# A new hand-set order of all engines, new PSUM banks and single-timed late weight loads in an attention and soft-MoE kernel

## Chip, cores and metric

The kernel runs on one core of one Trainium2 chip. The metric is device time in microseconds (us) of one execution; three executions of the kernel before gave a median of 356.9 us (354.47 to 360.94).

## What is computed

Eight batches with eight heads of 576 tokens and 64 channels go through block-causal attention (blocks of 64), and the result, as 4608 rows of 512, through a soft mixture of 8 experts with 4 slots each. All data are float32.

```python
scores = where(block_i >= block_j, q @ k.T / 8, -1e9)
x = softmax(scores) @ v                        # 4608 x 512
logits = x @ phi                               # 4608 x 32
slot_input = softmax(logits, axis=0).T @ x     # 32 x 512, over all rows
slot_out[e] = relu(slot_input[e] @ w1[e]) @ w2[e]
out = softmax(logits, axis=1) @ slot_out
```

The maximum over all rows makes a barrier: the experts start when the last batch has given its logits.

## The kernel before

**Two stages.** Stage one, up to about 299 us, is attention in 32 pairs of heads (4 pairs a batch, numbered 0 to 31) and, batch by batch, the logits and a running sum for the slots. Stage two, from `up` (L959) on, is the two expert layers and the output. The change touches stage one and the weight loads between the two.

**A pair.** The 576 rows of a pair's two heads are cut into tiles by how many key columns they may see: two tiles "7" of 512 columns (70 and 71, one for each head), two tiles "5" of 384 (50, 51), and the small ones "8" (576), "3" (256), "2" (192), "1" (128) and "0" (64). Its steps are:

- loads of k, q and v on SP (`load_k` L406, `load_q` L402, `load_v` L413 and L417), each into one of two areas that alternate by pair; k is scaled on POOL (L423)
- scores on PE: `qk` for the tiles 7 and 5 (L459), `qkb` for the others (L480)
- masked maximum on DVE (`rowmax`, L494 for tiles 7 and 5, L499 for the rest); exponential with its row sum on ACT (`expo`, L509)
- epsilon on POOL (`zeps`, L520) and reciprocal on DVE (`zinv`, L516), in three groups of tiles: 70 and 71, then 8 to 0, then 50 and 51; product with the reciprocal on POOL (`norm`, L527)
- 50 transposes on PE (`tr`, L547) in four groups g7 (16), g5 (12), gc (10, tile 8) and gd (12, tiles 3 to 0), each group into two PSUM banks, copied out by ACT (L389) or DVE (L391)
- product with v on PE (`pv` L579, `pv8` L589), copied out as x

**Once a batch.** PE makes the logits (L607, L614), 40 transposes of x (`xnat`, L716), 3 of the weights (`natural`, L666) and the slot sums (`slots` L736, `slots4` L745); POOL keeps the running maximum (L642, L645).

**What sets the order.** Every step is entered with a time, `at(t, fn, ...)`; the steps are sorted by time, and each engine gets its instructions in that order. The times are numbers in a table `TM` by step and place in the batch (`.0` to `.3`; letters for the first six and last three pairs). They only order; at run time an instruction goes when its semaphores allow, and an engine does not pass a waiting one. A table `EN` says which engine copies (v DVE, a ACT), a table `BK` which of the eight PSUM banks a step uses.

```python
  448          def scores(x, m):
...
  858          for t, _, fn, args in sorted(ops, key=lambda o: o[:2]):
  859              fn(*args)
```

**Weights.** 32 pieces of 1 MB. Pieces 0 to 16 go to places of their own during stage one, at times 1.6 pairs apart (L826). Pieces 17 to 23 (the late pieces) go over areas of attention that have ended (L846 to 854), the others over pieces that stage two has used.

Of the kernel before, what the change touches and what calls it, by code (L numbers as in the profile page):

```python
# [45 lines left out]
for name, n in (  # L46
# [58 lines left out]
    62.5406, "elg": 65.9472, "stats": 66.7664, "stats1": 67.0993, "stats2": 69.737, "enl": 82.2887, "ndt": 74.5616,  # L105
    "disp": 74.9226, "disp2": 135.6855, "xq0": 74.0947, "en0a": 75.0227, "en0b": 75.1964, "xq1": 62.9684, "en1a":
    65.1834, "en1b": 65.4166, "xn4": 65.4755, "en4a": 65.8907, "en4b": 65.8745, "sl": 90.1991, "sl4": 88.8341,
    "sacc": 91.9687, "sacc4": 90.0509, "lkA": -97.9102, "lqA": -56.266, "ksA": -73.6468, "lkB": -53.518, "lqB":
# [6 lines left out]
    -5.3661, "nm51A": -0.1355, "UBB": -7.3076, "gcA": 11.0108, "egcA": 13.7334, "ogcA": 13.9553, "rm8B": -6.9664,  # L115
# [6 lines left out]
    11.3725, "ex50B": 4.9925, "paA": 26.8907, "xbA": 26.6199, "ex51B": 4.1693, "xaA": 27.4575, "lqD": -20.3083,  # L122
# [128 lines left out]
def tile_attention_softmoe(  # L251
# [805 lines left out]
```

## Time and profile before

| what | value |
|---|---|
| median of three executions | 356.9 us (354.47 to 360.94) |
| profiled execution, its own time | 353.48 us |
| its span from first to last instruction | 351.4 us |
| PE busy | 333.5 us, 95% of the span |
| DVE, ACT, POOL busy | 269.8, 258.0, 205.9 us |
| mean granted TensorE clock | 0.992 |

Busy time is the union of an engine's instructions. A matmul's end is modelled, so the time from the start of one step to the start of the next says more than the length of a row. In the order lists below, one row is an instruction with its output, its input and the shape.

### The profile page before, as it was taken

How to read it: one execution, taken by the hardware profiler on the slowest of the kernel's cores; microseconds unless marked ns; L12 is line 12 of the kernel's file. 1: busy time of each engine (PE TensorE's matmuls, PEld its weight loads, DVE VectorE, ACT ScalarE, POOL GpSimd, SP SyncE). 2: the span in 40 equal slices, each digit the busy share in tenths (PEclk: the TensorE clock that was granted, in tenths of full speed). 3: DMA queues.
4: the chain of work that ended last, by engine and by line, in shares of the span. 5: the costliest groups of instructions: out<-in, count | busy, mean ns of one | idle time of the engine just before them, and what ended most of it. 6: DMA issues, size and time to landing. Idle time of an engine off the chain costs nothing.

```text
span 351.4 us, 14291 instructions
## 1 busy us (share of the span) xinstructions
PE 333.5 (95%) x5664; PEld 231.7 (66%) x5664; DVE 269.8 (77%) x816; ACT 258.0 (73%) x855; POOL 205.9 (59%) x475
## 2 busy tenths in 40 slices
PE   8899899999999999999999999799999999999990
PEld 4567577776767677768666777576767686347660
DVE  6899868989789869977898799678988856463352
ACT  4978968888988898878987898589878975032341
POOL 4887838867685768666866686567774862100000
PEclk9999999999999999999999999999999999999996
DMA  5766546385266453762565534823331139999988
GB/s 168 226 248 234 143 183 190 103 288 191 71 216 202 163 187 108 258 220 71 172 224 187 187 106 165 306 78 100 118 120 41 37 122 423 422 427 425 415 344 337
DMA packets 28930, 72.28 MB, mean 206 GB/s; under 512 B 6848, under 2 KB 15168, under 8 KB 23872
## 3 DMA queue, kind: packets, MB, share of 16 engines
q1 hardware_dynamic: 28864, 71.38, 57.1%
q8 instruction: 44, 0.72, 0.9%
q14 instruction: 22, 0.18, 0.1%
HBM read 61.93 MB, written 9.44 MB: 203 GB/s over the span
## 4 chain that ended last, share of the span: by engine, by line
PE 76%; DMA 7%; DVE 5%; POOL 5%; ACT 3%; issue 2%; SPq 1%; DVEq 0%; POOLq 0%
PE ps L579 16%; PE ps L547 14%; PE ps L459 12%; PE ps L480 8%; DMA arena<-in_v 6%; PE ps L589 5%; PE so L984 4%; PE hp L964 4%; POOL arena L527 4%; PE ps L716 3%; ACT arena L509 3%; PE o L935 3%; PE ps L607 2%; DVE ps L494 2%; PE ps L736 2%
## 5 line engine op out<-in xcount | busy, mean ns | idle before, releaser
L509 ACT ACTIVATE arena<-ps,stat 128x384 f32<-128x384 f32 (+6 forms) x288 | 152.7, 543 | 30.5 <-DVE stat L494 23.6
L527 POOL TENSOR_SCALAR arena<-arena,stat 128x384 f32<-128x384 f32 (+6 forms) x288 | 152.0, 544 | 31.4 <-DVE stat L516 19.6
L494 DVE CUSTOM_DVE_ANT_1 ps<-ps,mask 128x512 f32<-128x512 f32 (+1 forms) x128 | 76.5, 649 | 6.4 <-PE ps L459 5.1
L391 DVE COPY arena<-ps 128x384 f32<-128x384 f32 (+3 forms) x136 | 69.7, 548 | 15.1 <-PE ps L547 4.9
L579 PE MATMUL ps<-arena 128*64 128x256 f32 (+2 forms) x640 | 76.1, 384 | 2.7 <-DMA arena<-in_v 2.6
L389 ACT COPY arena<-ps 128x384 f32<-128x384 f32 (+3 forms) x140 | 62.7, 514 | 11.9 <-PE ps L547 7.6
L547 PE MATMUL ps<-ident,arena 64*128 64x64 f32 x1600 | 64.9, 227 | 1.7 <-POOL arena L527 0.9
L547 PEld LDWEIGHTS ps<-ident,arena 64*128 64x128 f32 x1600 | 57.0, 139 | 11.2 <-POOL arena L527 2.9
L579 PEld LDWEIGHTS ps<-arena 128*64 128x64 f32 x640 | 41.7, 137 | 32.9 <-issue 18.3
L509 ACT ACTIVATION_READ_ACCUMULATOR arena<-ps,stat 128x1 f32 x288 | 59.6, 207 | 0.0
L459 PE MATMUL ps<-arena 64*128 64x384 f32 (+1 forms) x256 | 58.7, 558 | 0.7 <-DMA arena<-in_q 0.4
L499 DVE TENSOR_REDUCE stat<-ps 128x1 f32<-128x128 f32 (+4 forms) x160 | 56.3, 401 | 3.4 <-PE ps L480 2.7
L480 PEld LDWEIGHTS ps<-arena 64*64 64x64 f32 x768 | 36.2, 132 | 21.1 <-ACT arena L389 8.6
L520 POOL TENSOR_SCALAR stat<-stat 128x2 f32<-128x2 f32 (+1 forms) x96 | 18.9, 197 | 48.5 <-ACT arena L509 44.5
L480 PE MATMUL ps<-arena 64*64 64x288 f32 (+4 forms) x768 | 42.9, 340 | 0.4 <-ACT arena L509 0.3
L459 PEld LDWEIGHTS ps<-arena 64*128 64x128 f32 x256 | 24.6, 187 | 15.2 <-issue 5.2
L589 PE MATMUL ps<-arena 128*64 128x64 f32 x640 | 24.9, 224 | 1.7 <-DMA arena<-in_v 1.7
L391 DVE COPY xn<-ps 128x512 f32<-128x512 f32 (+1 forms) x23 | 14.7, 650 | 13.0 <-ACT arena L509 11.7
L589 PEld LDWEIGHTS ps<-arena 128*64 128x64 f32 x640 | 22.3, 138 | 2.8 <-ACT arena L509 1.9
L423 POOL TENSOR_SCALAR arena<-arena 128x576 f32<-128x576 f32 x32 | 21.5, 673 | 3.6 <-DMA arena<-in_k 2.7
L945 DVE COPY arena<-o 128x512 f32<-128x512 f32 (+1 forms) x20 | 11.6, 632 | 11.9 <-PE o L935 11.9
L494 DVE DVE_READ_ACCUMULATOR2_ANT stat<- 128x1 f32 x128 | 18.0, 141 | 0.0
(115 smaller groups left out, 286.9 us busy)
## 6 DMA issues: line engine op xcount, KB each, us to landing
arena<-in_w SPq DMA_DIRECT2D x32, 1024.0 KB, 7.7
arena<-in_k SPq DMA_DIRECT2D x32, 288.0 KB, 3.4
arena<-in_q SPq DMA_DIRECT2D x32, 288.0 KB, 3.2
arena<-in_v SPq DMA_DIRECT2D x32, 256.0 KB, 4.2
out<-arena SPq DMA_DIRECT2D x7, 1024.0 KB, 5.5
out<-arena SPq DMA_DIRECT2D x4, 512.0 KB, 4.2
arena<-in_v SPq DMA_DIRECT2D x32, 32.0 KB, 3.8
arena<-in_phi SPq DMA_DIRECT2D x1, 64.0 KB, 2.7
```

Source lines behind the costliest of these rows:

```text
L389: nc.scalar.copy(out=out, in_=in_)
L391: nc.vector.tensor_copy(out=out, in_=in_)
L423: nc.gpsimd.tensor_scalar(out=area(f"ks{m % NQB}"), in0=area(f"ks{m % NQB}"), scalar1=SCALE, scalar2=0.0, op0=ALU.mult, op1=ALU.add)
L459: nc.tensor.matmul(scores(t + str(j), m), lhsT=q[r, lo:lo + 128], rhs=k[r, 0:NC[t]], start=True, stop=True)
L480: nc.tensor.matmul(o, lhsT=a, rhs=b, start=True, stop=True)
L494: nc.vector.tensor_tensor_reduce(out=sc, in0=sc, in1=ms, scale=-1.0, scalar=-NEG, op0=ALU.add, op1=ALU.min, accum_out=st[:, 0, COL[y]:COL[ ...
L499: nc.vector.tensor_reduce(out=st[:, 0, u:u + 1], in_=scores(x, m), axis=AX.XY if x == "8" else AX.X, op=ALU.max, negate=True)
L509: nc.scalar.activation(out=pr, in_=sc, func=AF.Exp, bias=st[:, 0, u:u + 1], accum_out=st[:, 1, u:u + 1], scale=-1.0 if x[0] in "75" else 1.0,)
L527: nc.gpsimd.tensor_scalar(out=pr, in0=pr, scalar1=st[:, 2, u:u + 1], scalar2=0.0, op0=ALU.mult, op1=ALU.add)
L547: nc.tensor.transpose(out=trbank(m, g)[i][:, 64 * n:64 * n + 64], in_=prob(m, x)[r, 128 * c:128 * c + 128], identity=ident[r, r],)
L579: nc.tensor.matmul(xps[m, 0][64 * j:64 * j + 64, lo:hi], lhsT=vs(m)[:, j, c, :], rhs=rhs, start=n == 0, stop=n == 4, skip_group_check=True,)
L589: nc.tensor.matmul(xps[m, 1][64 * j:64 * j + 64, 0:64], lhsT=vs(m)[:, j, c, :], rhs=arena[:, lo:lo + 64], start=(c == 0), stop=(c == NQ - 1),)
```

## The change

All numbers of `TM`, `EN` and `BK` are replaced: every engine gets another order, copies move between ACT and DVE, and each step has other banks. The maxima of tiles 50 and 51 become two entries with times of their own. The first clears (`pads`) get the time 0.0. The late pieces get times `P0z` to `P6z`.

```diff
 TM = {
-    "T": 8.6, "lk.0": -2.5895, "lq.0": 7.5732, "ks.0": 6.568, "lk.1": -4.2171, "lq.1": 6.1812, "UB.0": 9.8143,
...
+    "disp2z": 118.58, "xq0z": 113.5698, "en0az": 123.6836, "en0bz": 130.0397, "P0z": 81.8964, "P1z": 88.9749, "P2z":
...
-                xps["w"] = bank("pb")
+                xps["w"] = bank("pb", 0, ".0")
...
-            st, u = stat[m % 2], COL[x if x != "5" else "50"]
-            if x in "75" or x[0] == "7":
-                for y in ("50", "51") if x == "5" else (x,):
-                    n = NC[y[0]] // 2
-                    sc = scores(y, m).rearrange("p (a n) -> p a n", a=2)
...
+            st, u = stat[m % 2], COL[x]
+            if x[0] in "75":
+                n = NC[x[0]] // 2
+                sc = scores(x, m).rearrange("p (a n) -> p a n", a=2)
...
-            for x in ("70", "71", "8", "3", "2", "1", "0", "5"):
+            for x in COL:
                 at(t0 + tm(m, f"rm{x}"), rowmax, m, x)
-            for x in COL:
                 at(t0 + tm(m, f"ex{x}"), expo, m, x)
...
-        at(tm(0, "ks") + 0.001, pads, False)
+        at(0.0, pads, False)
...
-            places.append((max(ends[k] for k, (lo, hi) in AREAS.items() if lo < o + PIECE and hi > o), o))
-        last_v = end(NM - 1, ("lq", "lk", "lv"))
-        places = [(max(t, last_v + 0.001 * i), o) for i, (t, o) in enumerate(places)]
+            t = te + TM[f"P{o // PIECE}z"]
+            assert t > max(ends[k] for k, (lo, hi) in AREAS.items() if lo < o + PIECE and hi > o)
+            places.append((t, o))
         nxt = RES
-        for t, o in places:
-            at(t, load_piece, nxt, arena[:, o:o + PIECE])
+        for t, o in sorted(places):
+            at(t, load_piece, nxt, arena[:, o:o + PIECE], o // PIECE)
```

**Loads on SP near pair 23.** The queue before: the two loads of q for pairs 26 and 25, a weight piece, then v of pair 23 (two rows), k of pair 26, v of pair 24.

```order
L402 DMA arena<-in_q 128x576 x2
L330 DMA arena<-in_w 128x2048
L413 DMA arena<-in_v 128x2x256
L417 DMA arena<-in_v 64x2x64
L406 DMA arena<-in_k 128x576
```

The queue now: a weight piece, k of pair 25, v of pair 23, then q of pair 25 and k of pair 26.

```order
L333 DMA arena<-in_w 128x2048
L409 DMA arena<-in_k 128x576
L416 DMA arena<-in_v 128x2x256
L420 DMA arena<-in_v 64x2x64
L405 DMA arena<-in_q 128x576
L409 DMA arena<-in_k 128x576
```

The v of pair 23 has moved from behind q of pair 26 and a weight piece to just behind k of pair 25.

**Products on POOL for pair 10, after the running maximum of batch 1.** Before (128x256 is tile 3, 128x576 tile 8, 128x384 tile 51, 128x128 tile 1, 128x192 tile 2, 128x512 tiles 70 and 71, 128x64 tile 0; stat_108 is an epsilon of pair 11):

```order
L645 TENSOR_TENSOR bm_1673<-mrun_91,mrun_90 128x2
L527 TENSOR_SCALAR arena<-arena,stat_107 128x256
L527 TENSOR_SCALAR arena<-arena,stat_107 128x576
L527 TENSOR_SCALAR arena<-arena,stat_107 128x384
L527 TENSOR_SCALAR arena<-arena,stat_107 128x128
L527 TENSOR_SCALAR arena<-arena,stat_107 128x512
L527 TENSOR_SCALAR arena<-arena,stat_107 128x192
```

Now (L426 is the scaling of k for pair 12; tiles 1 and 2 have gone ahead of the first row):

```order
L647 TENSOR_TENSOR bm_1702<-mrun_91,mrun_90 128x2
L529 TENSOR_SCALAR arena<-arena,stat_107 128x384
L522 TENSOR_SCALAR stat_108<-stat_108 128x2
L426 TENSOR_SCALAR arena<-arena 128x576
L529 TENSOR_SCALAR arena<-arena,stat_107 128x512
L529 TENSOR_SCALAR arena<-arena,stat_107 128x576
L529 TENSOR_SCALAR arena<-arena,stat_107 128x64
L529 TENSOR_SCALAR arena<-arena,stat_107 128x256
```

Tile 0, which came last of all before (behind a second 128x512 and an epsilon), now comes sixth of the products and epsilons after the maximum; on PE its group gd, first of pair 10's four groups before, is now the last.

**Reciprocals on DVE for pair 8.** Before, the reciprocal of the five small tiles (128x5) and the first maximum of pair 9 behind it:

```order
L391 COPY arena<-ps 128x2x3x64
L391 COPY arena<-ps 128x384
L391 COPY arena<-ps 128x2x4x64
L391 COPY arena<-ps 128x320
L516 RECIPROCAL stat_107<-stat_107 128x5
L494 ISA ps,stat_108<-ps,mask 128x512
```

Now, with three masked maxima of pair 9 (a row each and a row that reads the result) and two plain ones ahead of it:

```order
L518 RECIPROCAL stat_107<-stat_107 128x2
L496 ISA ps,stat_108<-ps,mask 128x512
L496 ISA stat_108 128x1
L496 ISA ps,stat_108<-ps,mask 128x512
L496 ISA stat_108 128x1
L496 ISA ps,stat_108<-ps,mask 128x384
L496 ISA stat_108 128x1
L501 TENSOR_REDUCE stat_108<-ps 128x1 x2
L518 RECIPROCAL stat_107<-stat_107 128x5
```

The reciprocal for tiles 8 to 0 has moved behind five maxima of the next pair, the last of which (tile 8) needs the end of that pair's `qkb`.

## Rows read from the trace of the kernel before

**Rows 1.** Busy time by stretch: us, engines with counts, clock, DMA share, GB/s.

```profile
80.00:100.00 20.00, 20.00 (x364) 14.03 (x360) 16.76 (x56) 18.25 (x63) 14.46 (x35) 1.00 0.41 131
```

**Rows 2.** What PE waited for, whole span: us in total, times, longest.

```profile
PE ps L579 <- DMA arena<-in_v: 2.6, 2, 1.8
PE ps L589 <- DMA arena<-in_v: 1.7, 1, 1.7
```

**Rows 3.** SP in order of time, 205 to 226 us: start, length, DMA.

```profile
214.12 0.81 SPq L402 DMA_DIRECT2D arena<-in_q  x2
214.97 0.43 SPq L330 DMA_DIRECT2D arena<-in_w  x1
215.45 0.56 SPq L413 DMA_DIRECT2D arena<-in_v  x1
```

**Rows 4.** PE in order of time, 213 to 225 us; idle before in brackets.

```profile
212.73 1.32 PE L480 MATMUL ps<-arena 64*64 64x288 f32 x24
...
220.32 1.32 PE L480 MATMUL ps<-arena 64*64 64x288 f32 x24
223.47 1.73 PE L579 MATMUL ps<-arena 128*64 128x256 f32 x14 [1.83 <-DMA arena<-in_v]
```

**Rows 5.** PE in order of time, 153 to 200 us.

```profile
159.20 2.38 PE L579 MATMUL ps<-arena 128*64 128x256 f32 x20
...
173.72 0.41 PE L666 MATMUL ps<-ident,dt 64*128 64x64 f32 x3
173.96 1.36 PE L547 MATMUL ps<-ident,arena 64*128 64x64 f32 x38
175.26 1.77 PE L459 MATMUL ps<-arena 64*128 64x512 f32 x8
...
178.22 2.38 PE L579 MATMUL ps<-arena 128*64 128x256 f32 x20
...
181.11 2.08 PE L547 MATMUL ps<-ident,arena 64*128 64x64 f32 x50
...
189.02 0.43 PE L745 MATMUL ps<-xn,dn 128*32 128x128 f32 x8
...
190.34 1.79 PE L547 MATMUL ps<-ident,arena 64*128 64x64 f32 x50
191.96 1.82 PE L459 MATMUL ps<-arena 64*128 64x512 f32 x8
...
194.96 2.38 PE L579 MATMUL ps<-arena 128*64 128x256 f32 x20
197.27 1.08 PE L607 MATMUL ps<-xT,arena 128*32 128x128 f32 x32
...
198.73 0.71 PE L716 MATMUL ps<-ident,xT 64*128 64x64 f32 x16
```

**Rows 6.** Groups on DVE by shape: count, busy us, mean ns, idle before.

```profile
L499 DVE TENSOR_REDUCE stat<-ps 128x1 f32<-128x576 f32 x32 | 24.0, 750 | 2.9 <-PE ps L480 2.7
...
L499 DVE TENSOR_REDUCE stat<-ps 128x1 f32<-128x192 f32 x32 | 11.2, 349 | 0.4
...
L516 DVE RECIPROCAL stat<-stat 128x5 f32<-128x5 f32 x32 | 5.8, 181 | 0.5 <-POOL stat L520 0.4
```

**Rows 7.** Groups on POOL by shape, whole span.

```profile
L527 POOL TENSOR_SCALAR arena<-arena,stat 128x576 f32<-128x576 f32 x32 | 23.9, 746 | 5.3 <-PE ps L459 3.0 <-DVE stat L516 1.7
...
L527 POOL TENSOR_SCALAR arena<-arena,stat 128x256 f32<-128x256 f32 x32 | 15.3, 478 | 1.8 <-PE ps L459 0.4 <-DVE stat L516 0.4 <-PE ps L716 0.4
L527 POOL TENSOR_SCALAR arena<-arena,stat 128x192 f32<-128x192 f32 x32 | 13.6, 426 | 1.0
...
L527 POOL TENSOR_SCALAR arena<-arena,stat 128x128 f32<-128x128 f32 x32 | 11.9, 373 | 2.1 <-DVE stat L516 2.0
L527 POOL TENSOR_SCALAR arena<-arena,stat 128x64 f32<-128x64 f32 x32 | 10.2, 318 | 1.6 <-DVE stat L516 0.4
```

**Rows 8.** What PE waited for from 299 us to the end (first of three).

```profile
PE s_ps L910 <- DVE so_sb L990: 0.6, 2, 0.4
```

More of the change, by code (lines that the diff above doesn't have):

```diff
@@ L68 @@
 TM = {
[36 rows of a table removed]
[L105 to L108, printed above, removed]
[6 rows of a table removed]
-    -5.3661, "nm51A": -0.1355, "UBB": -7.3076, "gcA": 11.0108, "egcA": 13.7334, "ogcA": 13.9553, "rm8B": -6.9664,
[6 rows of a table removed]
@@ L122 @@
-    11.3725, "ex50B": 4.9925, "paA": 26.8907, "xbA": 26.6199, "ex51B": 4.1693, "xaA": 27.4575, "lqD": -20.3083,
[9 rows of a table removed]
-    "gcC": 21.5956, "egcC": 21.6353, "ogcC": 22.2453, "rm8D": 9.7444, "rm3D": 11.2045, "rm2D": 9.1358, "gdC":
[5 rows of a table removed]
-    "nm70D": 18.7307, "pvC": 28.6038, "lvD": 24.7104, "nm71D": 20.6412, "ex50D": 12.6593, "lkF": -5.5499, "paC":
-    29.9906, "xbC": 29.9765, "ex51D": 9.9732, "xaC": 30.5815, "ze2D": 18.7523, "lqF": -5.2021, "z2D": 19.3489,
-    "nm50D": 20.1939, "nm51D": 23.5913, "UBE": 8.8427, "gcD": 22.4032, "egcD": 22.7564, "ogcD": 23.2522, "rm8E":
[7 rows of a table removed]
@@ L148 @@
-    "z2E": 11.5496, "nm50E": 15.0918, "nm51E": 12.9825, "lgsu": 61.4744, "elgu": 62.5719, "UBF": 8.986, "gcE":
[9 rows of a table removed]
-    "nm50F": 16.9687, "nm51F": 20.665, "gcF": 24.444, "egcF": 25.0069, "ogcF": 25.4865, "gdF": 22.7904, "egdF":
-    24.1688, "ogdF": 25.6183, "g7F": 23.9349, "eg7F": 24.5587, "og7F": 24.338, "g5F": 22.2497, "eg5F": 23.4606,
-    "og5F": 22.6159, "xq1u": 62.4241, "en1au": 64.157, "en1bu": 64.1641, "xn4u": 64.732, "en4au": 65.5157, "en4bu":
-    65.9659, "pvF": 27.7516, "paF": 30.3892, "xbF": 29.3666, "xaF": 31.1866, "slu": 89.7423, "sl4u": 90.5393,
@@ L162 @@
-    "saccu": 91.8489, "sacc4u": 91.9606, "lkx": -0.9869, "lqx": -6.1222, "ksx": 1.9972, "lkw": -2.4657, "lqw":
[8 rows of a table removed]
-    27.576, "UBw": 8.6552, "gcx": 28.6017, "egcx": 29.6287, "ogcx": 29.8666, "rm8w": 8.6568, "rm3w": 12.5678,
[8 rows of a table removed]
-    "nm51w": 30.9679, "UBy": 17.1802, "gcw": 41.9368, "egcw": 47.0796, "ogcw": 47.5157, "rm8y": 18.3266, "rm3y":
[6 rows of a table removed]
-    "pvw": 48.1646, "lvy": 48.433, "nm71y": 40.2511, "ex50y": 22.1806, "paw": 48.1974, "ex51y": 21.7154, "xbw":
-    55.8751, "xaw": 55.9008, "ze2y": 22.6711, "z2y": 38.979, "nm50y": 39.22, "nm51y": 47.9333, "gcy": 42.1474,
@@ L189 @@
-    "egcy": 48.0716, "ogcy": 47.0108, "gdy": 47.4013, "egdy": 53.3148, "ogdy": 51.9444, "g7y": 44.5797, "eg7y":
-    48.0396, "og7y": 50.0656, "g5y": 48.6367, "eg5y": 51.6982, "og5y": 51.3296, "pvy": 54.4458, "pay": 50.7838,
-    "xby": 57.7544, "xay": 51.9204, "lgsz": 83.9316, "elgz": 97.7368, "statsz": 89.6525, "stats1z": 90.1069,
[5 rows of a table removed]
[39 rows of a table added]
+    "lkA": -137.7828, "lqA": -130.1467, "ksA": -68.3295, "lkB": -55.4774, "lqB": -50.0018, "UBA": -40.5202, "rm8A":
[6 rows of a table added]
+    1.4658, "UBB": -5.4494, "gcA": 10.1958, "egcA": 12.0994, "ogcA": 12.3861, "rm8B": -1.3742, "rm3B": 1.7296,
[6 rows of a table added]
@@ new lines @@
+    16.8155, "ex50B": 4.1603, "paA": 24.5255, "xbA": 25.1142, "ex51B": -0.5744, "xaA": 25.5728, "lqD": 0.2222,
[7 rows of a table added]
+    24.1802, "lvC": 13.0386, "nm71C": 13.1681, "ex50C": 6.5922, "lkE": -8.277, "paB": 25.8725, "xbB": 25.8512,
+    "ex51C": 6.8775, "xaB": 26.1172, "lqE": -9.3457, "ze2C": 8.9248, "z2C": 11.4725, "nm50C": 14.4335, "nm51C":
+    16.3082, "UBD": 4.7553, "gcC": 17.4608, "egcC": 18.2277, "ogcC": 18.5974, "rm8D": 5.1022, "rm3D": 9.602, "rm2D":
[6 rows of a table added]
+    8.4801, "lkF": -10.6889, "paC": 19.4522, "xbC": 25.0432, "ex51D": 7.3327, "xaC": 20.4851, "ze2D": 9.8191, "lqF":
[9 rows of a table added]
@@ new lines @@
+    4.0959, "gcE": 17.9387, "egcE": 18.5212, "ogcE": 19.8555, "rm8F": 4.8382, "rm3F": 7.522, "rm2F": 4.8677, "gdE":
[8 rows of a table added]
+    "z2F": 11.1101, "nm50F": 12.4738, "nm51F": 16.5266, "gcF": 15.0882, "egcF": 16.2853, "ogcF": 16.5725, "gdF":
+    17.5768, "egdF": 18.8138, "ogdF": 18.5547, "g7F": 17.2596, "eg7F": 17.6316, "og7F": 18.2673, "g5F": 17.5577,
+    "eg5F": 21.126, "og5F": 18.681, "xq1u": 65.0625, "en1au": 65.385, "en1bu": 65.9459, "xn4u": 62.9896, "en4au":
+    65.016, "en4bu": 65.2076, "pvF": 24.4174, "paF": 25.9486, "xbF": 24.6661, "xaF": 26.0784, "slu": 73.079, "sl4u":
@@ new lines @@
+    72.4763, "saccu": 77.2326, "sacc4u": 72.7774, "lkx": -10.2471, "lqx": -10.417, "ksx": 1.4167, "lkw": -8.6929,
+    "lqw": -11.6916, "lgsv": 70.2465, "elgv": 70.3576, "UBx": 3.7596, "rm8x": 3.9614, "rm3x": 4.6004, "rm2x":
[7 rows of a table added]
+    "nm51x": 16.2374, "UBw": 4.0398, "gcx": 18.1469, "egcx": 20.6286, "ogcx": 18.8398, "rm8w": 4.8599, "rm3w":
[8 rows of a table added]
+    "nm50w": 31.1513, "nm51w": 37.8388, "UBy": 15.2566, "gcw": 50.2747, "egcw": 52.0434, "ogcw": 52.2908, "rm8y":
[8 rows of a table added]
+    "nm51y": 46.0497, "gcy": 46.6026, "egcy": 49.283, "ogcy": 53.4725, "gdy": 56.4664, "egdy": 56.4788, "ogdy":
@@ L197 @@
+    57.8677, "g7y": 36.3496, "eg7y": 46.0185, "og7y": 47.9302, "g5y": 48.084, "eg5y": 56.318, "og5y": 50.7279,
+    "pvy": 58.9265, "pay": 57.7938, "xby": 61.3379, "xay": 63.4045, "lgsz": 94.5153, "elgz": 142.3154, "statsz":
+    97.2378, "stats1z": 97.3265, "stats2z": 101.5187, "enlz": 144.8707, "ndtz": 118.354, "dispz": 128.2055,
[6 rows of a table added]
 }
 EN = {
[17 rows of a table removed]
[16 rows of a table added]
 }
@@ L221 @@
 BK = {
[12 rows of a table removed]
-    (3, 0), "g5F": (2, 0), "gcA": (1, 5), "gcB": (2, 1), "gcC": (5, 2), "gcD": (5, 4), "gcE": (6, 2), "gcF": (6, 0),
-    "gdA": (0, 7), "gdB": (7, 6), "gdC": (4, 7), "gdD": (0, 6), "gdE": (4, 3), "gdF": (1, 7), "pbB": (0,), "pbC":
-    (6,), "pbD": (5,), "pbE": (1,), "paA": (4,), "paB": (7,), "paC": (4,), "paD": (4,), "paE": (7,), "paF": (5,),
[4 rows of a table removed]
-    "gcy": (1, 5), "gdw": (7, 4), "gdx": (4, 6), "gdy": (6, 2), "pbw": (0,), "pbx": (3,), "pby": (4,), "paw": (7,),
-    "pax": (5,), "pay": (1,), "lgv": (4,), "lgz": (1,), "xq0v": (3, 7), "xq0z": (5, 6), "xq1v": (7, 5), "xq1z": (2,
-    3), "xn4v": (1, 2), "xn4z": (4, 0), "ndv": (6, 2), "ndz": (7, 2), "slv": (6,), "slz": (6,), "sl4z": (1,), "pb":
-    (2,), "B21": (0,), "A70": (2,),
[14 rows of a table added]
+    "g5F": (7, 5), "gcA": (7, 4), "gcB": (1, 6), "gcC": (7, 3), "gcD": (4, 6), "gcE": (4, 3), "gcF": (2, 4), "gdA":
+    (1, 3), "gdB": (0, 5), "gdC": (2, 4), "gdD": (5, 3), "gdE": (2, 0), "gdF": (2, 6), "pbA": (7,), "pbB": (5,),
+    "pbC": (2,), "pbD": (3,), "pbE": (7,), "pbF": (0,), "paA": (4,), "paB": (2,), "paC": (7,), "paD": (1,), "paE":
[4 rows of a table added]
+    "gcw": (5, 4), "gcx": (3, 0), "gcy": (0, 2), "gdw": (4, 3), "gdx": (6, 2), "gdy": (3, 5), "pbw": (7,), "pbx":
+    (1,), "pby": (2,), "paw": (5,), "pax": (7,), "pay": (1,), "lgv": (3,), "lgz": (2,), "xq0v": (5, 6), "xq0z": (6,
+    7), "xq1v": (0, 1), "xq1z": (5, 3), "xn4v": (4, 7), "xn4z": (1, 4), "ndv": (7, 6), "ndz": (2, 1), "slv": (5,),
+    "slz": (5,), "sl4z": (1,),
 }
@@ L326, in tile_attention_softmoe, with load_piece @@
     place = {}
-    def load_piece(i, dst):
+    def load_piece(i, dst, at=0):
         place[i] = dst
@@ L486, in rowmax @@
         def rowmax(m, x):
-            st, u = stat[m % 2], COL[x if x != "5" else "50"]
-            if x in "75" or x[0] == "7":
-                for y in ("50", "51") if x == "5" else (x,):
-                    n = NC[y[0]] // 2
-                    sc = scores(y, m).rearrange("p (a n) -> p a n", a=2)
-                    ms = mask[:, 256 - n:256]
-                    ms = bass.AP(tensor=ms.tensor, offset=ms.offset, ap=[list(ms.ap[0]), [64, 2], [1, n]])
-                    nc.vector.tensor_tensor_reduce(
-                        out=sc, in0=sc, in1=ms, scale=-1.0, scalar=-NEG, op0=ALU.add, op1=ALU.min,
-                        accum_out=st[:, 0, COL[y]:COL[y] + 1],
-                    )
+            st, u = stat[m % 2], COL[x]
+            if x[0] in "75":
+                n = NC[x[0]] // 2
+                sc = scores(x, m).rearrange("p (a n) -> p a n", a=2)
+                ms = mask[:, 256 - n:256]
+                ms = bass.AP(tensor=ms.tensor, offset=ms.offset, ap=[list(ms.ap[0]), [64, 2], [1, n]])
+                nc.vector.tensor_tensor_reduce(
+                    out=sc, in0=sc, in1=ms, scale=-1.0, scalar=-NEG, op0=ALU.add, op1=ALU.min,
+                    accum_out=st[:, 0, u:u + 1],
+                )
             else:
```

280 rows, old and new, of tables (BK, EN, TM) are left out of this document.

## Prediction

> **What bounds the kernel now.** I read the busy time by stretch first: between 80 and 100 us PE is busy for 20.00 of 20 us at a granted clock of 1.00, while DVE has 14.03, ACT 16.76 and POOL 18.25 [rows 1]. So PE is the bound of stage one, and since the change leaves PE's instructions as they are (the same steps, in another order), it can gain or lose only where PE stands still or lets a group drag because an operand is late. Two views tell how much that is. The first is the list of what PE waited for: the loads of v stand there with 2.6 us in two waits at `pv` and 1.7 us in one at `pv8`, 4.3 us in all [rows 2]. Other waits it names are shorter and spread over copies and products.
>
> The second is PE in order of time, read from start to start, because a group of fifty transposes whose products arrive late appears as one long row and not as a wait. In batch 4, `pv` of pair 16 starts at 159.20 and `pv` of pair 20 at 194.96, a period of 35.76 us. Against it I set each step where it ran without a pause [rows 5]: `pv` with its neighbour 178.22 to 181.11 = 2.89; fifty transposes 190.34 to 191.96 = 1.62; the three score groups 175.26 to 178.22 = 2.96. Four pairs of these are 4 x 7.47 = 29.88. Once a batch come the logits, 197.27 to 198.73 = 1.46; the slot sums, 189.02 to 190.34 = 1.32; the three transposes of the weights, 173.72 to 173.96 = 0.24; and 40 transposes of x, at the rate of the fifty, 1.30. Together 34.20. So some 1.56 us of each batch is hidden waiting. Five batches run in this steady order, so there are about 7.8 us beside the 4.3 in stage one (an estimate; the fastest stretches needn't all be reachable together).
>
> **The loads of v.** The worst case is pair 23. SP, which issues in order, had q of a later pair at 214.12, a weight piece at 214.97 and only then v at 215.45 [rows 3]. That q waits until the scores of pair 24, which read the area, are done: their last group starts at 212.73 and takes 1.32, so ends at 214.05 [rows 4]. PE could have begun pair 23's `pv` at 220.32 + 1.32 = 221.64, 7.6 us later, but resumed at 223.47, with 1.83 us of wait on in_v [rows 4]. From issue to use the v behind a weight piece thus took 8.0 us. The Trainium skill, "DMA: Bandwidth & Descriptors", section "Where 436 GB/s comes from", puts the fabric's ceiling at about 435 GB/s, from which 1 MB alone would take an estimated 2.4 us; by that this wait would vanish with any small lead, and the 8.0 us of this trace, with several loads in flight, says it would not; the sum goes by the 8.0.
>
> In the new order v of pair 23 goes ahead of q of pair 25 and needs only the end of `pv` of pair 21; that is one pair's steps earlier. A pair takes 35.76 / 4 = 8.9 us. Walking PE's new order with the durations above gives leads of about 13.6 us for pair 23 and its like, and 10.4 us for the tightest pairs (those that still stand behind a q), against the 8.0 needed: 2.4 to spare. I take all 4.3 us as gone; at worst none goes (the tight class waits instead), and more than 4.3 can't go by this.
>
> **The order on PE, DVE, ACT and POOL, and the banks.** They aim at the same 1.56 us a batch. From above, all 7.8 go. From below, the new order brings as many late operands as it removes and the term is nothing: in it the products have new neighbours too, and a group of scores that wants a bank must wait for a copy that another engine now makes. By the same walk most margins are 0.3 to 0.4 us, the length of one product of 64 to 128 columns, 0.318 to 0.373 [rows 7], so a few will fail. I take the middle, 3.9 gone, since no row of before decides between the ends. Tile 0's product, last of the pair before and now in the middle, is one such move: with its group gd last on PE it has more time, not less.
>
> **The two maxima of tile 5.** They were already two instructions for each pair; two entries allow another place, not other work. Price nothing. DVE has 269.8 us busy of a span of 351.4 and covers the few copies that move to it (about 0.65 us a batch by the shapes moved); were that cover gone, 7 x 0.65 = 4.6 us would be the worst.
>
> **Clears, first pairs.** They move within the head, where PE waits for the first loads. The walk gives the first `pv` at the old time within 0.3 us; I take 0, and at most one group of scores, 1.32 [rows 4], either way.
>
> **Late weight pieces.** In the order of SP none of them goes ahead of the last v, before or now; the times only place them behind it. In stage two PE's longest listed waits, 0.6 us in two, are for a copy and not for in_w [rows 8]. So nothing hangs on when they land: 0. If they came later and stage two did wait, the wait would be of a piece's 8.0 us less what the first expert group covers; I keep 1 us for it.
>
> **The end of stage one.** The slot sums of batch 6 now stand ahead of the logits of batch 7. They fill PE while it would wait for the last copies, so 0; if they delay the logits, and with them the barrier, the whole 1.32 us [rows 5] comes on top, and as much could be gained where they left an emptier end behind.
>
> **The sum.** -4.3 - 3.9 + 0 + 0 + 0 = -8.2 us against the profiled execution's own 353.48, which gives 345.3. The median of the three runs is 356.9, 3.4 above that execution; the same difference on the median gives 348.7.
>
> **Rivals.**
>
> *All waits go.* The order reaches the floor of 34.20 a batch: -4.3 - 7.8 = -12.1, 344.8. For it speaks that PE alone bounds the stretch and that the other engines have slack [rows 1]; against it, that POOL has only 1.75 us in 20 and that the margins are one small product wide.
>
> *New waits for old.* Only the loads' 4.3 goes: 352.6. For it: these same margins, and the period of before was near its floor, 4% above it. Against it: nothing in the new order that I could name pays for all of 7.8.
>
> *The reciprocals come late: slower.* The reciprocal of the small tiles (128x5) now stands on DVE behind five maxima of the next pair, and these read the scores. Count from the start of that pair's last score group: it ends at 1.32 [rows 4], two maxima and the reciprocal take 0.349 + 0.750 + 0.181 [rows 6], so 2.60; then POOL makes five products, 0.746 + 0.373 + 0.426 + 0.478 + 0.318 = 2.34 [rows 7], so 4.94. PE gets to gd after the score group, `pv` and its neighbour, and 38 of 50 transposes: 1.32 + 2.89 + 1.23 = 5.44 [rows 4, 5]. The spare is 0.5 us. If DVE reaches the maxima 1.5 us late, as two copies between them would make it, PE waits 1.0 us in each of two pairs a batch, from seven batches 14, and with the loads' 4.3 gone that is +9.7: 366.6. It decides from 0.5 us of lateness on. Before, the reciprocal stood ahead of these maxima; DVE lost just 0.5 us before it and POOL's 128x128 product 2.0 us [rows 6, 7], so the place was not free of waits then either. Against it: DVE is idle 6 of 20 us [rows 1]. The Trainium skill, "PSUM — Partial Sum Buffer", section "Engine vs sequencer instructions", says that the queues of ScalarE, VectorE and GpSimd are strictly first in, first out; it speaks for this rival, as a reciprocal whose own inputs are ready can't pass a maximum that waits, and no row of before shows DVE passing one.
>
> *It does not do what it says.* For the late pieces ahead of the last values this is so by the order; its term is 0 in every case, and the forecast stands without it.
>
> **How the numbers follow.** The forecast gets 0.40, all waits gone 0.22, new waits for old 0.31, late reciprocals 0.07. The time is the forecast's, 348.7. The range reaches on the fast side past 344.8 by the head's and tail's bounds together, 2.7, so 342; on the slow side it takes in 352.6 and those 2.7, and 1 for the late pieces, and about half a microsecond for the spread between runs, so 357; it leaves out the late reciprocals and a tail of the others. A difference of 2% is about what can be told from none here: 356.9 x 0.98 = 349.8. The forecast lies just beyond it, so its 0.40 goes 0.25 to faster and 0.15 to same; with 0.22 of the first rival faster is 0.47; the second makes same 0.46; the last is slower, 0.07.
>
> **What would show it right or wrong.** In the profile after: the waits of PE at the `pv` lines for in_v should be gone, with v of pair 23 issued about 13 us ahead of its use; the period from pair 16's `pv` to pair 20's should be near 35.0 (34.2 for the first rival, 35.8 for the second); DVE's idle before the 128x5 reciprocal should stay near 0.5 and PE's waits for POOL at the transposes (L549 there) small, else the slower rival holds; stage two should keep its length. Wrong it is if v waits show at other pairs, or if the period does not fall while the copies of scores' banks appear in PE's list of waits.

## The result, and the profile after

The changed kernel takes 344.27 us, the median of four executions (343.46 to 345.85), against 356.86 for the kernel before (354.47 to 360.94). The ratio is 0.967, with a 95% interval of 0.961 to 0.974: 11.6 us less. (The ratios leave disturbed executions out, the medians don't; theirs differ by 12.6.) The profiled execution took 343.54 us, 9.9 less than that of before; its span is 341.8 us. The prediction was 348.7 with a range of 342 to 357; the measured time lies in the range, close to the rival "all waits go" (344.8).

The page, first lines: PE's share of the span has gone from 95 to 96%, at the same count of instructions.

```profile
span 341.8 us, 14324 instructions
...
PE 327.4 (96%) x5664; PEld 230.6 (67%) x5664; DVE 272.6 (80%) x821; ACT 257.3 (75%) x850; POOL 205.7 (60%) x475
```

What PE waited for, whole span of the changed kernel (us in total, times, longest), which answers to [rows 2]:

```profile
PE ps L433 <- DVE zrun L292: 0.9, 1, 0.9
PE ps L549 <- ACT arena L511: 0.8, 1, 0.8
PE ps L766 <- DVE acc L761: 0.6, 1, 0.6
PE s_ps L911 <- DVE so_sb L991: 0.6, 2, 0.4
PE ps L549 <- POOL arena L529: 0.6, 2, 0.3
```

No row with in_v is left, neither for the large product (now L581) nor for tile 8's (L591). The reason is read from SP between 186 and 218 us, which answers to [rows 3] (start, length, DMA):

```profile
199.10 0.33 SPq L409 DMA_DIRECT2D arena<-in_k  x1
201.81 0.56 SPq L416 DMA_DIRECT2D arena<-in_v  x1
202.46 0.56 SPq L420 DMA_DIRECT2D arena<-in_v  x1
203.07 0.58 SPq L405 DMA_DIRECT2D arena<-in_q  x1
```

and from PE in order of time, which answers to [rows 4, 5]:

```profile
154.26 2.38 PE L581 MATMUL ps<-arena 128*64 128x256 f32 x20
...
188.53 2.38 PE L581 MATMUL ps<-arena 128*64 128x256 f32 x20
...
206.87 1.32 PE L483 MATMUL ps<-arena 64*64 64x288 f32 x24
...
214.46 1.32 PE L483 MATMUL ps<-arena 64*64 64x288 f32 x24
215.71 2.38 PE L581 MATMUL ps<-arena 128*64 128x256 f32 x20
```

v of pair 23 goes out at 201.81, between k and q of pair 25, and is used at 215.71, 13.9 us later; the last row has no bracket, so PE did not wait. The first two rows are `pv` of pairs 16 and 20: the period is 34.27 us, against 35.76 before, and against the 34.20 that the steps take without a pause. By the same reading the five steady batches from pair 8 to pair 28 take 34.25 to 35.27 us each, 34.56 in the mean, against 35.61 to 37.24 before, 36.06 in the mean (two of the waits for v are in that).

Where the 9.6 us of the span went, from start to start on PE in the two profiled executions: the first `pv` comes 0.64 us sooner (18.78 for 19.42); from there to `pv` of pair 31 it is 259.71 us for 270.08, 10.37 less; from there to the first expert matmul 11.46 for 11.14, 0.32 more; and from that to the end 51.81 for 50.77, 1.04 more. The last is the writing of the output: PE's last matmul ends 42.7 us after the first expert matmul in both. Whether it belongs to the change is not shown, but it may: the end comes 50.8 to 51.4 us after the first expert matmul in the kernel before and the six made from it below, and 51.7 to 53.7 in the changed kernel and the six made from that.

### The profile page after: what moved, and what is told of

It is laid out like the page before. It is cut to its first block, busy times and chain, and to the rows that moved or that the text cites. A ratio compares the mean times of both kernels' runs of the same rounds, so it can differ in the third digit from the quotient of the medians.

```text
span 341.8 us, 14324 instructions
## 1 busy us (share of the span) xinstructions
PE 327.4 (96%) x5664; PEld 230.6 (67%) x5664; DVE 272.6 (80%) x821; ACT 257.3 (75%) x850; POOL 205.7 (60%) x475
## 4 chain that ended last, share of the span: by engine, by line
PE 89%; DVE 3%; POOL 2%; DMA 2%; issue 1%; ACT 1%; DVEq 0%; SPq 0%; POOLq 0%
PE ps L581 21%; PE ps L549 16%; PE ps L462 14%; PE ps L483 11%; PE ps L591 5%; PE so L985 4%; PE hp L965 4%; PE o L936 3%; PE ps L718 2%; PE ps L609 2%; PE ps L738 2%; DMA arena<-in_k 2%; POOL arena L529 1%; PE ps L433 1%; PE ps L616 1%; PE ps L747 1%
## 5 line engine op out<-in xcount | busy, mean ns | idle before, releaser
L529 POOL TENSOR_SCALAR arena<-arena,stat 128x512 f32<-128x512 f32 (+6 forms) x288 | 152.0, 545 | 16.8 <-DVE stat L518 13.3
L496 DVE CUSTOM_DVE_ANT_1 ps<-ps,mask 128x384 f32<-128x384 f32 (+1 forms) x128 | 77.7, 636 | 6.8 <-PE ps L462 5.6
L394 DVE COPY arena<-ps 128x384 f32<-128x384 f32 (+3 forms) x134 | 68.5, 557 | 10.9 <-PE ps L549 4.8
L581 PE MATMUL ps<-arena 128*64 128x256 f32 (+2 forms) x640 | 76.1, 384 | 0.0
L392 ACT COPY arena<-ps 128x384 f32<-128x384 f32 (+3 forms) x142 | 65.2, 495 | 12.3 <-PE ps L549 8.9
L549 PE MATMUL ps<-ident,arena 64*128 64x64 f32 x1600 | 61.5, 226 | 1.8 <-ACT arena L511 0.8
L501 DVE TENSOR_REDUCE stat<-ps 128x1 f32<-128x64 f32 (+4 forms) x160 | 58.1, 404 | 6.0 <-ACT arena L511 3.7
L581 PEld LDWEIGHTS ps<-arena 128*64 128x64 f32 x640 | 40.9, 136 | 31.7 <-issue 18.8
L462 PE MATMUL ps<-arena 64*128 64x384 f32 (+1 forms) x256 | 60.6, 562 | 0.3 <-ACT arena L511 0.3
L426 POOL TENSOR_SCALAR arena<-arena 128x576 f32<-128x576 f32 x32 | 21.5, 672 | 6.7 <-DMA arena<-in_k 5.3
L591 PE MATMUL ps<-arena 128*64 128x64 f32 x640 | 24.3, 222 | 0.0
L591 PEld LDWEIGHTS ps<-arena 128*64 128x64 f32 x640 | 22.6, 138 | 0.4
L394 DVE COPY xT<-ps 128x512 f32<-128x512 f32 (+1 forms) x27 | 15.3, 581 | 9.2 <-PE ps L581 8.8
L946 DVE COPY arena<-o 128x512 f32<-128x512 f32 (+1 forms) x20 | 11.6, 632 | 11.9 <-PE o L936 11.9
```

The source lines that it names most:

```text
L392: nc.scalar.copy(out=out, in_=in_)
L394: nc.vector.tensor_copy(out=out, in_=in_)
L426: nc.gpsimd.tensor_scalar(out=area(f"ks{m % NQB}"), in0=area(f"ks{m % NQB}"), scalar1=SCALE, scalar2=0.0, op0=ALU.mult, op1=ALU.add)
L462: nc.tensor.matmul(scores(t + str(j), m), lhsT=q[r, lo:lo + 128], rhs=k[r, 0:NC[t]], start=True, stop=True)
L496: nc.vector.tensor_tensor_reduce(out=sc, in0=sc, in1=ms, scale=-1.0, scalar=-NEG, op0=ALU.add, op1=ALU.min, accum_out=st[:, 0, u:u + 1],)
L501: nc.vector.tensor_reduce(out=st[:, 0, u:u + 1], in_=scores(x, m), axis=AX.XY if x == "8" else AX.X, op=ALU.max, negate=True)
```

## The experiments

Twelve kernels ran. Those made from the kernel before are compared with its runs on the same chip at the same time (ratios), those made from the changed kernel with its 344.27.

**1. v far ahead, in the kernel before (e1_v_early).** It takes one part of the change alone, the loads of v.

```diff
-"lv.3": 26.2329, "lvD": 24.7104
+"lv.3": 14.2,    "lvD": 12.5
```

> The kernel before, with one edit: v of every fourth pair (3, 7, ... 27) is issued on SP ahead of the q of later pairs and the weight piece it stood behind. My theory: PE's waits for in_v (4.3 us in before's trace: pairs 3, 15, 23) go, nothing else changes: span 351.4 to about 347.1, time 4.3 us below before. Rival 1 (they hide other waits): the waits move to another releaser, span within 1 us of before. Rival 2 (the spread of before's runs, 354.5 to 360.9, is made by these loads): the median falls by more, 6 to 7 us, and the runs lie within 2 us of each other.

Measured: 378.94 us, ratio 1.067 (1.061 to 1.073), 24 us slower. Neither theory nor rival. The list of PE's waits has no in_v any more, but (whole span of this kernel):

```profile
PE ps L459 <- DMA arena<-in_q: 17.8, 7, 4.3
PE ps L459 <- POOL arena L423: 3.2, 2, 3.0
```

I had put v ahead of a load too many. SP at pair 11:

```profile
100.46 0.34 SPq L406 DMA_DIRECT2D arena<-in_k  x1
104.17 0.55 SPq L413 DMA_DIRECT2D arena<-in_v  x1
104.82 0.56 SPq L417 DMA_DIRECT2D arena<-in_v  x1
105.43 0.58 SPq L402 DMA_DIRECT2D arena<-in_q  x1
```

From 100.8 to 104.17 SP stands at v, which must not overwrite the area of pair 9 before its tile 8 product is done, and q of pair 12, whose own area was free, goes out only at 105.43. PE in order of time then shows the scores of pair 11 undisturbed, the tile 8 product of pair 9, and the scores of pair 12:

```profile
97.37 1.74 PE L459 MATMUL ps<-arena 64*128 64x512 f32 x8
...
103.44 0.80 PE L589 MATMUL ps<-arena 128*64 128x64 f32 x20
...
109.75 2.84 PE L459 MATMUL ps<-arena 64*128 64x512 f32 x8 [3.42 <-DMA arena<-in_q]
112.52 1.89 PE L480 MATMUL ps<-arena 64*64 64x288 f32 x24
```

There is a second cost beside the wait of 3.42: the same eight matmuls take 2.84 us instead of 1.74. The stretches (us; busy time of PE, PEld, DVE, ACT, POOL with counts; granted clock; DMA share; GB/s) say why:

```profile
107.00:109.00 2.00, 0.00 (x0) 0.00 (x0) 0.25 (x2) 0.32 (x1) 1.93 (x4) 1.00 0.94 217
109.00:111.00 2.00, 1.25 (x4) 0.66 (x6) 0.00 (x0) 0.00 (x0) 0.20 (x1) 0.83 1.02 332
111.00:113.00 2.00, 2.00 (x11) 0.79 (x11) 1.61 (x5) 0.82 (x3) 0.00 (x0) 0.50 0.62 258
113.00:115.00 2.00, 2.00 (x30) 1.73 (x24) 1.32 (x7) 1.79 (x6) 0.32 (x2) 0.82 0.05 16
115.00:117.00 2.00, 2.00 (x32) 1.32 (x30) 1.45 (x6) 1.85 (x8) 1.86 (x5) 1.00 0.71 197
```

PE did nothing from 106.3 to 109.75, and behind that the granted clock fell from 1.00 to 0.50, the lower of its two levels (1.2 of 2.4 GHz), before it came back. So this wait is paid about one and a half times: 3.42 us, and 1.7 more in the scores. It is not so for every wait: behind the one of 2.99 us for POOL at pair 24 the clock stayed at 1.00.

**2. Tile 0's product sooner, in the kernel before (e2_tile0_early).** It takes one part of the new order on POOL.

```diff
-"nm2.2": 19.4852, "nm0.2": 20.0564
+"nm2.2": 18.9609, "nm0.2": 18.961
```

> The kernel before, with one edit: on POOL the products of tiles 2 and 0 of every fourth pair (6, 10, ... 26) go ahead of the two 128x512 products, so that the first group of transposes, gd, finds them. Theory: in before gd starts 0.36 to 0.62 us ahead of the end of tile 0's product in six pairs (2.9 us in all), while the other three groups have 3 to 6 us to spare, so the order of these products is the greatest hidden wait: about -2.9 us (span near 348.5). Rival: the lateness passes on to the group g7, whose products come 0.75 us later, or to the pair behind: within 1 us of before.

Measured: 351.84 us, ratio 0.990 (0.986 to 0.994), 3.5 us faster (2.0 to 4.9). The theory holds.

**3. Both edits of 1 and 2 (e5_both).**

> The kernel before with both edits, v of every fourth pair earlier on SP and the products of tiles 2 and 0 earlier on POOL. If the two waits are independent the gains add: 4.3 + 2.9 = 7.2 us, span near 344.2, which would leave 2.4 us of the changed kernel's 9.6 (of the span) to all the rest. If one wait covers the other, no more than 5 us.

Measured: 376.26 us, ratio 1.055 (1.045 to 1.065). It carries the same mistake as the first and settles nothing but that the second edit is worth about as much there (2.7 us).

**4. v behind its place, in the changed kernel (e3_v_late).**

```diff
-"lv.3": 13.3142
+"lv.3": 25.85
```

> The changed kernel, with v of every fourth pair (7, 11, ... 27) put back behind q of a later pair and, where one is due, the weight piece. In the changed kernel's PE order pair 23's turn comes 7.5 us after the scores that release that q; before, v took 8.0 us from issue to use behind a piece. Theory: waits for in_v return at the pairs with a piece ahead, 0.5 to 2 us each in two or three pairs: +1 to +4 us against the changed kernel (343.5 profiled), about 346. Rival (the order of the transposes has made the place harmless): within 0.5 us of it.

This kernel takes part of the computation away: by its time the load stands behind the product that uses it, so the products of pairs 7, 11, ... 27 use the v of the pair two before and wait for no load. Measured: 345.03 us. It tells nothing of the wait; it shows only that the load's later place on SP delays nothing else by more than a microsecond.

**5. v ahead of one q only, in the kernel before (f1_v_ahead_q).** It mends the first.

```diff
-"lv.3": 26.2329, "lvD": 24.7104
+"lv.3": 19.1,    "lvD": 19.9
```

> The kernel before, with one edit: v of every fourth pair (3, 7, ... 27) goes on SP just ahead of the q that waits for the next score group (q of pair 26 for v of pair 23) and of the weight piece, but stays behind the loads that stood before that q; so SP waits for pair 21's product with v, which ends at 209.0, while that q would wait until 214.05. Theory: the waits for in_v (4.3 us) go and no q is held up: span near 347.1, time 4 us below before; if the spread of before's runs comes from these loads, the runs also lie within 2 to 3 us and the median falls by 6. Rival: the waits were a cover for others: within 1 us of before.

Measured: 349.55 us, ratio 0.984 (0.980 to 0.989); the span is 347.3. The span of the profiled execution is 4.1 us shorter, as the 4.3 in [rows 2] say, and its own time 3.6; by the ratio it is 5.6 (3.9 to 7.3). The four runs lie between 349.16 and 349.91, the runs of before that the ratio uses between 353.3 and 356.5. The theory holds; that the spread of before's runs comes from these loads (rival 2 of experiment 1) has the narrow spread on its side, but not more than that. SP of this kernel, beside [rows 3], and PE's scores of pair 24:

```profile
206.27 0.55 SPq L413 DMA_DIRECT2D arena<-in_v  x1
206.92 0.56 SPq L417 DMA_DIRECT2D arena<-in_v  x1
211.46 0.81 SPq L402 DMA_DIRECT2D arena<-in_q  x2
```

```profile
210.07 1.32 PE L480 MATMUL ps<-arena 64*64 64x288 f32 x24
```

v of pair 23 is out 5.2 us ahead of the q that it stood behind, and that q still goes out at the end of the scores of pair 24 (211.39). What is left at the head of PE's list is the product of experiment 2:

```profile
PE ps L547 <- POOL arena L527: 1.2, 4, 0.4
```

**6. The mended edit and experiment 2's (f2_both).** The two diffs of 5 and 2 together.

> The kernel before with the v loads ahead of that q, and on POOL the products of tiles 2 and 0 ahead of the two of 128x512 in every fourth pair (6, 10, ... 26). Independent waits: 4.3 + 2.9 to 3.5 = 7 to 8 us below before, median 348 to 349, which leaves 4 us or less of the change's 12 to all the rest of the new order. If one covers the other: 351 or more.

Measured: 347.53 us, ratio 0.980 (0.974 to 0.986): 7.2 us (5.1 to 9.3) faster than before, and 2.0 below the loads' edit alone. Each edit alone had brought 5.6 and 3.5, so the sum is 9.1; the intervals leave open whether the two are independent or overlap by a part. Neither covers the other. Two edits of four numbers bring 7.2 of the 11.6 us; 3.3 remain between this kernel's median and the changed one's (the 7.2 and the 11.6 come from different runs of the kernel before, so they do not add up to the microsecond).

**7. q and a weight piece ahead of v, in the changed kernel (f3_v_behind).**

```diff
-"lq.2": -1.528
+"lq.2": -12.84
...
-at((4 + 3.2 * i) / 2 * T, load_piece, ...)
+at((4 + 3.2 * i) / 2 * T + 1.1, load_piece, ...)
```

> The changed kernel with q of every fourth pair (10, 18, 26) moved to just ahead of v of the pair three before it, where it waits for the scores that release its area, and all weight pieces 1.1 units later, so that one stands between this q and the v in pairs 7, 15 and 23: the queue order of before in the order of after. The scores of pair 24 end at 208.2, so v of pair 23 is issued near 209.2 and by the 8.0 us of before is there at 217.2; PE's turn is at 215.7. Theory: about 1.5 us of wait for in_v in each of three pairs, +4.5 us against the changed kernel (bounds +2 to +6). Rival: without effect, as v then comes in less time: within 0.7 us.

Measured: 365.97 us, ratio 1.029 to before, 21.7 us slower than the changed kernel. The mechanism is that of experiment 1 and not the one I meant:

```profile
PE ps L462 <- DMA arena<-in_q: 15.0, 6, 3.4
```

The q that was moved waits on SP for the scores that release its area, here q of pair 26 for those of pair 24, and q of pair 25 stands behind it, a weight piece and v of pair 23:

```profile
227.68 0.33 SPq L405 DMA_DIRECT2D arena<-in_q  x1
228.06 0.42 SPq L333 DMA_DIRECT2D arena<-in_w  x1
228.53 0.56 SPq L416 DMA_DIRECT2D arena<-in_v  x1
229.14 0.61 SPq L420 DMA_DIRECT2D arena<-in_v  x1
229.80 0.60 SPq L405 DMA_DIRECT2D arena<-in_q  x1
```

PE in order of time has the last scores of pair 24, which end at 227.61, and the first of pair 25:

```profile
226.29 1.32 PE L483 MATMUL ps<-arena 64*64 64x288 f32 x24
...
234.85 1.77 PE L462 MATMUL ps<-arena 64*128 64x512 f32 x8 [2.46 <-DMA arena<-in_q]
```

So q of pair 25, which the changed kernel issues 9.7 us ahead of its scores (203.07 for 212.75), goes out 5.1 us ahead of them here, and PE waits. No wait for in_v appears, so the 1.5 us a pair were not tested.

**8. The reciprocals late, in the changed kernel (f4_z_late).**

```diff
-"z1.0": 14.4753
+"z1.0": 15.6
```

> The changed kernel with the reciprocal of the small tiles of pairs 8, 12, ... 28 behind five more instructions on DVE (a masked maximum with its result, two plain maxima, another reciprocal: about 1.4 us later). In the changed kernel's trace gd of these pairs starts within 0.1 us of the end of its last product, so there is no spare. Theory (late reciprocals price): 6 pairs x 1.4 = +8 us, if POOL makes the products as much later; bounds +4 to +9. Rival: POOL was busy with other products at that time and PE has other transposes to do: under +2 us.

Here, too, part of the computation falls away: by its time the reciprocal now stands behind the product of tile 8, which so takes the row sum itself instead of its reciprocal and does not wait for it. Measured: 345.58 us; as a price of lateness it says nothing. Experiment 9 mends it.

**9. The reciprocals late, with the products behind them (g1_z_late).**

```diff
-"z1.0": 14.4753, "rm1.1": 6.7843, "z0.1": 6.966, "rm3.1": 8.6985
+"z1.0": 15.3,    "rm1.1": 6.65,   "z0.1": 6.69,  "rm3.1": 6.66
```

> The changed kernel with the reciprocal of the small tiles of pairs 8, 12, ... 28 some 1.4 us later on DVE: a masked maximum, three plain maxima and another reciprocal of the next pair now stand ahead of it. In the changed kernel POOL begins the first of the five products 0.8 us after that reciprocal's end (it makes another epsilon first), and gd starts within 0.1 us of the last product. Theory (no spare at gd): the products start 0.6 to 0.9 us later and PE waits as long in each of six pairs: +3.5 to +5.5 us, with PE's waits for POOL at the transposes in the profile. Rival (PE or the copies are behind anyway): within 0.7 us of the changed kernel (344.3).

Measured: 346.84 us (346.66 to 348.55), 2.6 us above the changed kernel. For the products of pair 16, POOL in the changed kernel and here:

```profile
148.66 2.24 POOL L529 TENSOR_SCALAR arena<-arena,stat 128x576 f32<-128x576 f32 x5
```

```profile
149.91 2.24 POOL L529 TENSOR_SCALAR arena<-arena,stat 128x576 f32<-128x576 f32 x5 [0.74 <-DVE stat L518]
```

and PE's transposes of that pair in this kernel:

```profile
150.71 1.90 PE L549 MATMUL ps<-ident,arena 64*128 64x64 f32 x50 [0.41 <-POOL arena L529]
```

POOL now waits 0.74 for the reciprocal, and PE 0.41 for POOL. In five of the six pairs the step ahead of these transposes is 0.48 us longer to the next start, 2.4 us in all: the mechanism of my slower rival, at somewhat under the price expected.

**10. The late pieces by the old rule (g2_pieces_old).**

```diff
-t = te + TM[f"P{o // PIECE}z"]
+t = max(ends of the areas it covers, last_v + 0.001 * i)
```

> The changed kernel with the seven late weight pieces entered by the old rule (as soon as the area is free, behind the last v) instead of times of their own. On SP the order of the kinds of loads stays the same, only which area a piece fills at which turn differs. My prediction put this part at 0: within 0.5 us of the changed kernel (344.3, span 341.8, first expert matmul to end 51.9 us). Rival: the times let the pieces start sooner, and old times cost up to 1 us at stage two's start, with a wait of PE for in_w.

Measured: 344.09 us, 0.2 below the changed kernel, within the spread. No wait for a piece is among PE's waits in stage two. By the median the part is worth nothing either way. The profiled execution has two differences that cancel: from the first `pv` to that of pair 31 it is 1.4 us shorter than in the changed kernel's, and from the first expert matmul to the end 53.0 us, 1.2 longer. As experiment 9, which keeps the new times, also has 52.6 there, the 1.2 can't be put down to the old rule.

**11. k ahead of the weight piece, in the changed kernel (g3_k_early).** An attempt to beat it.

```diff
-"lk.0": -5.3461
+"lk.0": -11.6
```

> The changed kernel with k of every fourth pair (8, 12, 16, ... 28) just ahead of the weight piece and the two loads of v that it stood behind. In the changed kernel's trace POOL waits 1.2 us for k of pair 16, behind two products of pair 14, and PE then waits 0.97 us at pair 14's second group of transposes. Theory: that wait goes and nothing else moves: 0.8 to 1.2 us below the changed kernel, about 343.2. Rival: the weight piece and the v loads behind k come later and give it back: within 0.4 us of it or slower.

Measured: 344.32 us: no gain. The wait for k is gone, and v of pair 13, now behind k and the piece, is late in its place (PE in order of time):

```profile
133.13 2.38 PE L581 MATMUL ps<-arena 128*64 128x256 f32 x20 [1.81 <-DMA arena<-in_v]
```

The DMA view gives issue to landing for these loads (count, KB, us): the stretch 120.4 to 121.8 of the changed kernel, then 122.5 to 123.7 of this one.

```profile
arena<-in_v SPq DMA_DIRECT2D x1, 256.0 KB, 7.5
```

```profile
arena<-in_v SPq DMA_DIRECT2D x1, 256.0 KB, 10.4
```

The rival holds. In the changed kernel this v is issued at 120.49 and used at 129.38, 8.9 us with 7.5 needed.

**12. Tile 8's product beside the others, on top of 6 (g4_pa_next).** It takes a part of PE's new order alone.

```diff
-"pa.0": 31.4003, "pa.1": 31.0946
+"pa.0": 27.933,  "pa.1": 28.2741
```

> The kernel before with both edits (v ahead of q, products of tiles 2 and 0 earlier) and, in half of the pairs, tile 8's product with v directly behind the pair's other products instead of behind logits and transposes. In the profiles a product with v takes 2.21 us to the next start where the next step is of its own kind and 2.31 where it is not, and tile 8's 0.68 instead of 0.73; the changed kernel always has them side by side, and its steady batches are 0.6 us shorter than those of both edits together. Theory (PE loses a little at each change of kind of step): 0.25 to 0.5 us a batch, 2 to 3.5 us below the 347.5 of both edits. Rival: only the label of the time changes, as the transposes then follow another kind: within 0.7 us of it.

Measured: 354.79 us, 7.3 slower than experiment 6. From start to start the products did what was expected: per batch the four `pv` take 8.84 us instead of 9.04 and the four `pv8` 2.72 instead of 2.83, as in the changed kernel (8.84 and 2.74). The Trainium skill says that a change of tiling mode drains TensorE ("TensorEngine Tiling (Array Packing)", section "Key Properties"); the 0.10 and 0.05 us here fit it, as `pv` and `pv8` share 128*64 and their other neighbours do not. But PE's list of waits fills up:

```profile
PE ps L716 <- DVE arena L391: 3.3, 5, 0.7
PE ps L547 <- ACT arena L389: 1.8, 7, 0.3
PE ps L547 <- ACT arena L509: 1.1, 6, 0.2
```

Logits, transposes of x and transposes of the products now come sooner against copies that DVE and ACT still make in their old order, and the gain of 0.30 a batch is paid back several times: from start to start the transposes of x alone take 3.00 us in the batch from pair 16, against 1.46 in experiment 6.

## Why the prediction was right, and where it was not

The direction, the cause and the range held; the forecast's 8.2 us fell short of 11.6 by 3.4, in two terms.

**What bounds the kernel: right, from a row read one column off.** In [rows 1] the second figure, 14.03, is PE's weight loads; DVE has 16.76, ACT 18.25 and POOL 14.46. That PE is the bound stands. Two arguments built on the other figures do not: it was ACT and not POOL that had only 1.75 us to spare in 20, while POOL had 5.5, so one of the two reasons against "all waits go" was void; and DVE was idle for 3.2 us of 20 and not for 6, which made the case against the late reciprocals weaker than it read.

**The loads of v: right in place, too small on the median.** "I take all 4.3 us as gone": gone they are, and experiment 5 shows that the queue's order alone does it. But the term was read from one execution, and the step "the same difference on the median" took over whatever that execution happened to show: the change gained 9.9 us in the profiled executions and 11.6 over the runs. Experiment 5 has a like gap, 3.6 by own time (4.1 by the span) against 5.6, and a narrower spread, which points to these loads; its interval reaches down to 3.9, so it is not settled.

**The hidden waits: the term that was mis-sized.** "I take the middle, 3.9 gone, since no row of before decides between the ends." More went: between the first `pv` and that of pair 31 the profiled execution lost 10.37 us, of which 4.3 were the loads, so 6.1 of the 7.8. A comparison in before's trace would have decided a part of it. In pairs 6, 10, ... 26 gd, the first of its pair's groups, starts 0.4 to 0.6 us ahead of the end of its last operand, tile 0's product, and drags until it is there, while the products of the other three have been ready for 3 to 6 us when PE comes to them. For pair 10 of the kernel before, gd and the step behind it on PE, and tile 0's product on POOL:

```profile
99.76 0.87 PE L547 MATMUL ps<-ident,arena 64*128 64x64 f32 x12
100.56 0.80 PE L589 MATMUL ps<-arena 128*64 128x64 f32 x20
```

```profile
99.86 0.32 POOL L527 TENSOR_SCALAR arena<-arena,stat 128x64 f32<-128x64 f32 x1
```

and the same two steps of PE in experiment 6:

```profile
97.94 0.58 PE L547 MATMUL ps<-ident,arena 64*128 64x64 f32 x12
98.45 0.80 PE L589 MATMUL ps<-arena 128*64 128x64 f32 x20
```

Before, the product ends at 100.18, and gd takes 0.80 us to the next start; with the product moved it takes 0.51. That is an order gone wrong, not an engine at its limit, and an order can be put right whole. The prediction named this very move of tile 0 but gave it no price. Experiments 2 and 6 price it at 3.5 and 2.0 us; the forecast's 3.9 stood for this and all the rest of the order.

That rest, from experiment 6 to the changed kernel, measured 3.3. In the batch from pair 16 it is 0.90 us of PE's steps (35.17 to 34.27): 0.37 in the transposes of the products, and 0.29 in `pv` and `pv8`. So not all of the 1.56 us that I called waiting was that: 0.31 of it lies in `pv` and `pv8`, which waited for nothing and go faster beside each other (experiment 12 shows its size, and that it can't be had without the copies' order). Which of the moved products, copies and banks brings the 0.37 is not settled; old banks or old copy engines in the new order were not tried. What was left above the floor varies by batch: the longest, 35.27 from pair 12, has the wait for k that experiment 11 takes away.

**The slower rival: the mechanism is real, its spare was less.** I worked out 0.5 us of spare at gd. In the changed kernel's trace gd starts within 0.1 us of the end of the last of the five products in pairs 8, 12, ... 24, and the first group, gc, 0.1 to 0.2 us behind the product of tile 8 that it needs. Experiment 9 adds 1.4 us on DVE and PE pays 0.4 to 0.5 a pair. The change stays just on the safe side; the place that waits first is gc and not gd, as POOL makes the product of 128x576 first. The two signs that the prediction named for this rival stayed small: DVE is idle for 0.6 us in all before the 128x5 reciprocals, and PE waits 0.6 us for POOL at the transposes.

**The lead of v: one pair right, the tight class too high.** 13.6 us were worked out for pair 23 and 13.9 measured. For the tight class it was 10.4 against 8.0 needed; measured, pairs 9, 13, ... 25 have 8.9 to 9.8 from issue to use. The tightest, pair 13, has 8.9 against 7.5, and experiment 11 shows that one load more in front makes the 7.5 into 10.4 and costs 1.8 us. "8.0" is no constant but grew with what was queued ahead.

**Head, tail, late pieces, maxima.** Head 0 (bounds 1.3): it was -0.64. The end of stage one 0: +0.32. Stage two was to keep its length: it took 1.04 more, at the writing of the output, and why is open. Late pieces 0: right on the median by experiment 10. The two maxima of tile 5 were not tried alone; nothing in PE's waits points to them.

## What to carry to other kernels

Before asking which engine is at its limit, set each group's start against the time at which each of its operands was ready: one group that waits while its neighbours have been ready for microseconds is an order to be changed, and four numbers here (two of them for the loads) gave nearly two thirds of the gain of a whole new order. A load that waits on an in-order queue should wait behind nothing that waits longer, and hold up nothing that is due sooner: the same v moved a little brings 5.6 us, and moved a little too far costs 24. A gain read from one profiled execution should be given with the gap between that execution and the other runs, as both may shrink together.

## What the runs showed of the hardware that I had not expected

A stall of PE can cost more than its length: behind the 3.42 us wait in experiment 1 the granted clock fell to 0.50, and the scores that followed took 1.1 and 0.6 us more. Behind the 2.99 us wait in the same kernel, and the waits of 1.7 and 1.8 us in the kernel before, it stayed at 1.00.

A load's time from issue to landing behind one 1 MB piece was 7.5, 7.9 and 10.4 us in three kernels, with different loads in flight.

In some executions PE stands still once for 1.4 to 1.9 us for nothing that the profile shows. In experiment 6 it is 1.7 us among the transposes of pair 21:

```profile
PE ps L547 <- issue: 1.7, 1, 1.7
```

Experiments 2, 7 and 11 show one elsewhere, 1.9, 1.4 and 1.6 us. In all four a packet of 16 KB on the queue that the profile calls instruction starts 0.3 to 1.0 us ahead of the stall. Such packets come about 7 us apart all through, mostly without a stall, so this is a hint and not a cause; what it is stays open.
